# A chunked mLSTM with a four-expert layer behind it: small moves between engines and queues in the recurrence

## The chip, the cores and the metric

The kernel runs on one core of one Trainium2 chip. The metric is the device time of one execution in microseconds (us); lower is better. Three executions of the kernel before took 395.02, 394.61 and 394.67 us, median 394.67. One further execution was profiled.

## The reference

The first half is an mLSTM: for 2 batches and 8 heads, over 768 steps, with head size 40. With a running maximum m of the log gates:

```
m_new  = max(f + m, i);  fs = exp(f + m - m_new);  is = exp(i - m_new)
C = fs * C + is * v k^T;   n = fs * n + is * k
y = sigmoid(o) * (C q) / max(|n . q|, 1)
```

The 16 heads' outputs of a step are joined to a row x of 320 numbers; there are 1536 rows. The second half sends every row through four experts and adds them up with weights p, where p = domain_probs / (sum of domain_probs over the experts + 1e-9):

```
out = sum over e of  p[:, e] * (max(x @ w1[e], 0) @ w2[e])      # w1: 320 x 1024, w2: 1024 x 320
```

All is float32. The experts' matmuls keep that precision by splitting both operands into a high and a low part of a faster format and adding three products.

## The kernel before

The sequence is cut into 6 chunks of 128 steps, and one "pair" j is chunk j of both batches (n = 2j and 2j+1). Inside a chunk from the second on, the work goes in halves of 64 steps. The state of all heads is carried from half to half in small tiles cs. Each pair passes through the same functions:

- load_qk, load_vk, load_o and load_f fetch q and k, v and k, the output gates, and the forget factors, the last broadcast to 64 partitions from a copy in HBM, f_d. gate_o takes the sigmoid of the output gates, in place, on ScalarE.
- decay scans the factors to decay products (VectorE, L432); scores makes q.k (TensorE, L479); weigh multiplies both (VectorE, L497).
- values and keys scale v and k on GpSimd (L454, L458); state multiplies them on TensorE (L527); carry (GpSimd, L534) and keep (VectorE, L543) bring the state forward.
- inter multiplies q with the carried state (TensorE, L554) and scales the product by a factor of its row and head to yb; intra multiplies the weighed scores with v (L595).
- norms adds yb to intra's result in PSUM (L602), multiplies with the output gates (L606), divides (L610, L611 and L646 to L653); turn transposes the rows (TensorE, L661), and the result is split to high and low parts in xst (ScalarE L664, VectorE L668).

steps(n) interleaves n pieces of expert 0's matmuls (hidden, L157; output, L204) with this recurrence. After it the four experts run as a long stream of matmuls on TensorE, with 512 rows at a time, while the next expert's weights are loaded and split.

Every engine works through its own instructions in the order in which the Python code issues them; nothing is reordered. All loads and stores are issued from SyncE (SP), in code order too. A load that shall not start too early is held back by behind(ap): a tiny store to a scratch row `mark`, which waits until ap has been written, and everything after it on SP waits with it. Each transfer uses one of eight semaphores in turn, and waits until the transfer eight before it has landed.

The places touched by the change: the tile f_d (L266), its two stores (L770 to L774) and its reading (load_f, L428); the load of the domain weights pw (L775), their sum (L827 to L831) and their scaling (L849, L852); the load of the third pair's output gates (L819) and their sigmoid (L918); inter's scaling on VectorE, used for pair 1 only (L559 to L565); the scan of n = 5 (decay(5), L889), its keys (L890) and the mark before load_f(3) (L891).

Of the kernel before, what the change touches and what calls it, by code (L numbers as in the profile page):

```python
# [44 lines left out]
def tile_mlstm_moe(ctx, tc, g0, g1, qk, vk, ot, dp, w1, w2, out):  # L45
# [177 lines left out]
    with ExitStack() as actx:  # L223
# [39 lines left out]
        gl = gp.tile([L, S], F32, name="gl")  # L263
        tri = const.tile([L, 2, L], F32, name="tri")
        half = const.tile([L, 32], F32, name="half")
        f_d = dram.tile([B, 2 * (NC - 2), H * C], F32, name="f_d")  # L266
        mark = dram.tile([24, 32], F32, name="mark")
        marks = iter(range(24))
        ident = const.tile([L, L], F32, name="ident")
# [105 lines left out]
        def load_qk(j, c=None):  # L375
            c = slice(0, 2) if c is None else slice(c, c + 1)
            nc.sync.dma_start(qks[j % 2][:, c], qk[j, :, c])
# [7 lines left out]
        def load_o(j):  # L385
            nc.sync.dma_start(acc[:, 2 * j:2 * j + 2], ot[:, 2 * j:2 * j + 2])
# [34 lines left out]
        def load_f(j):  # L421
            for n in (2 * j, 2 * j + 1):
                b, c = n % B, n // B
                fbs[n] = fb = a0.tile([L, H, C], F32, tag="fb", name="fb")
                for u in range(2):
                    nc.sync.dma_start(
                        fb[hs[u]].rearrange("p h t -> p (h t)"),
                        f_d[b, 2 * (c - 2) + u:2 * (c - 2) + u + 1].to_broadcast([C, H * C]),  # L428
                    )

        def scan(out, f, i):
# [25 lines left out]
        def keys(n):  # L457
            nc.gpsimd.tensor_mul(  # L458
                kp[n % 2][:, :, 0:D], vks[n // 2][:, n % 2, 1],
                dds[n][:, :, (C if n // B else L) - 1:].to_broadcast([L, H, D]),  # L460
            )
# [49 lines left out]
        def cst(j, u):  # L511
            return cs[(2 * j + u) % 3]
# [19 lines left out]
        def carry(j, u):  # L532
            cd = cds[j, u] = a1.tile([104, B * NP, D + 1], F32, tag=f"cd{u}", name="cd")
            nc.gpsimd.tensor_mul(  # L534
                cd, cst(j, u)[0:104],
                bl[0:104, u, j].unsqueeze(2).to_broadcast([104, B * NP, D + 1]),
            )

        def keep(j, u):

            st, cd = sts[j][u], cds.pop((j, u))
            for q in rows:
                nc.vector.tensor_add(cst(j, u + 1)[q], cd[q], st[q, :, 0:D + 1])  # L543

        def inter(j, eng=nc.scalar):

            y1 = ps_a.tile([L, 2, B, NP, C], F32, tag="a", name="y1")
            for n in (2 * j, 2 * j + 1):
                b = n % B
                for p in range(NP):  # L550
                    for r in range(2):
                        q = slice(64 * r, 64 + D * r)
                        for u in (r, 1 - r):
                            nc.tensor.matmul(  # L554
                                y1[hs[u ^ r], r, b, p, 0:D + 1], qT(n)[q, p, hs[u]],
                                cst(j, u)[q, b * NP + p], start=True, stop=True,
                            )
            yb = ybs[j] = a1.tile([L, 2, B, NP, D + 1], F32, tag="yb", name="yb")
            if eng is nc.vector:  # L559
                eng.tensor_mul(  # L560
                    yb.rearrange("t r b p d -> t r (b p) d"),
                    y1.rearrange("t r b p d -> t r (b p) d")[..., 0:D + 1],
                    bT[:, :, j].unsqueeze(3).to_broadcast([L, 2, B * NP, D + 1]),
                )
                return  # L565
            for b in range(B):
                for p in range(NP):
                    for r in range(2):
                        i = b * NP + p
                        nc.scalar.activation(  # L570
                            yb[:, r, b, p], y1[:, r, b, p, 0:D + 1], AF.Copy,
                            scale=bT[:, r, j, i:i + 1],
                        )

        def intra0(b):
            pool, tag = (ps_a, "a") if b else (ps_h, "ph")
            y = ys[0, b] = pool.tile([L, 2, NP, C], F32, tag=tag, name="y0")
            for p in range(NP):
                for r in range(2):
                    h = 2 * p + r  # L580
                    for t in hs:
                        nc.tensor.matmul(
                            y[t, r, p, 0:D + 1], pms[b][:, h, t], vp[b][:, h, 0:D + 1],
                            start=True, stop=True,
                        )
# [107 lines left out]
        def decays(j):  # L693
            decay(2 * j)
            decay(2 * j + 1)
            if j + 1 < NG:
                load_f(j + 1)
# [3 lines left out]
        def steps(n):  # L701
            for _ in range(n):
                if not work[0].step():
                    work.pop(0)
# [62 lines left out]
        scores(1)  # L767
        gate_o(0)
        gate_starts(2, nc.gpsimd)
        for b in range(B):  # L770
            nc.sync.dma_start(  # L771
                f_d[b].rearrange("u (h t) -> h u t", h=H),
                fs[b * H:(b + 1) * H].rearrange("h (u t) -> h u t", t=C),
            )  # L774
        nc.sync.dma_start(pw, dp)  # L775
        load_w1(1)
        load_vk(1)
        load_qk(1, 1)
        intra0(0)
        quarter_hi(0)  # L780
        decay(1)
# [34 lines left out]
        )  # L816
        load_f(2)
        load_o(1)
        load_o(2)  # L819
        scores(3)  # L820
        values(2)
        keys(2)
# [1 line left out]
        quarter_lo(3, nc.vector)  # L824
        weigh(1)
        values(3)
        psum_e = const.tile([L, NCH, 1], F32, name="psum_e")  # L827
        nc.gpsimd.tensor_add(psum_e, pw[:, :, 0:1], pw[:, :, 1:2])
        for e in range(2, NE):
            nc.gpsimd.tensor_add(psum_e, psum_e, pw[:, :, e:e + 1])  # L830
        nc.gpsimd.tensor_scalar_add(psum_e, psum_e, 1e-9)  # L831
        keys(3)
        gate_b(1, NC, ps_o.tile([L, 512], F32, tag="po", name="pb"))
        bexp(1, NC)
# [11 lines left out]
        split_w2_lo(w2s, 4, 2, w2r, nc.gpsimd)  # L846
        state(1)
        keep(1, 0)
        nc.vector.reciprocal(psum_e, psum_e)  # L849
        carry(1, 1)  # L850
        split_w2_lo(w2s, 6, 2, w2r, nc.gpsimd)
        nc.gpsimd.tensor_mul(pw, pw, psum_e.to_broadcast([L, NCH, NE]))  # L852
        steps(1)
        gate_o(1)
        keep(1, 1)
# [7 lines left out]
        for j in range(1, NG):  # L863
            a, b = 2 * j, 2 * j + 1
            nxt, far = j + 1 < NG, j + 2 < NG
            k = SLOTS[j - 1]
            if j == NG - 2:
                raw1 = raws.tile([L, 3, FF], F32, tag="raw", name="raw1")

            def load(i, ap):  # L870
                if far or j == NG - 2:
                    behind(ap)
                if far:
                    (load_vk, None, lambda j: (load_qk(j), load_o(j)))[i](j + 2)
                elif j == NG - 2:
                    nc.sync.dma_start(raw1[:, i], w1[1, :, i])

            if nxt:
                values(a + 2)
                values(b + 2)  # L880
                if j > 1:
                    decays(j + 1)
                keys(a + 2)
                if j > 1:
                    keys(b + 2)
                steps(1)
            norm = norms(j)
            if j == 1:
                decay(5)  # L889
                keys(5)  # L890
                behind(dds[5][0:1, 0, 0:32])  # L891
                load_f(3)
            else:
                load(0, xms.pop(j)[0:1, 1, 0, 0:32])
                steps(1)
            norm(nc.vector if j == 1 else nc.gpsimd)
            if j == 1:
                steps(1)
            if nxt:
                carry(j + 1, 0)  # L900
            if j == 1:
                scores(a + 2)
                scores(b + 2)
                weigh(j + 1)
            steps(k[0] - 1 - nxt)
            if j > 1:
                turn(j)()
            if nxt:
                if j > 1:
                    gate_o(j + 1)  # L910
                if j > 1:
                    scores(a + 2)
                    scores(b + 2)
                hidden = work[0].todo[0][0] == work[0].hidden
                state(j + 1, *((ps_o, "po") if hidden else (ps_h, "ph")))
                if j == 1:
                    low = turn(j)
                    gate_o(j + 1)  # L918
                keep(j + 1, 0)
                if j == 1:  # L920
                    load(0, cst(j + 1, 1)[0:1, 0, 0:32])
                if not far:
                    load(1, cst(j + 1, 1)[0:1, 0, 0:32])
                low() if j == 1 else weigh(j + 1)
                if far:
                    carry(j + 1, 1)
                    keep(j + 1, 1)
                steps(k[1])
                inter(j + 1)
                load(2, ybs[j + 1][0:1, 0, 0, 0, 0:32])  # L930
                intra(j + 1)
# [113 lines left out]
```

## Time and profile before

| what | value |
|---|---|
| median of three executions | 394.67 us (394.61 to 395.02) |
| the profiled execution, its own time | 393.91 us |
| its span, first to last instruction | 392.3 us |
| mean granted TensorE clock | 0.998 |
| TensorE matmul (PE) busy | 385.1 us, 98% |
| TensorE weight load (PEld) busy | 350.7 us, 89% |
| VectorE (DVE), ScalarE (ACT), GpSimd (POOL) busy | 158.0, 122.1 and 93.9 us |
| transfers of queue q1 (data), q8 (instructions) | 27.95 MB, 0.46 MB |

Start times are counted from the first instruction of the span. The busy time of PE is modelled at its ends, so a busy PE may be a little less busy than the row says. "<-" in a row names what ended a wait; "issue" is a wait that ends with nothing that the profile records. The recurrence lies in the first 107 us; from there on the four experts' stream follows.

### The profile page before, as it was taken

The numbers are of one execution on the slowest core, as the hardware profiler recorded it, in microseconds if no ns is written. First come the engines' busy times: TensorE is split into PE (matmuls) and PEld (weight loads), VectorE is DVE, ScalarE is ACT, GpSimd is POOL, SyncE is SP. The second block draws the span as 40 slices with busy tenths as digits, with TensorE's granted clock in tenths as the row PEclk, the third lists the DMA queues.
The fourth block names the chain that finished last, engine by engine and source line by source line (L and its number), as shares of the span: only waits on it lengthen the run. The fifth ranks groups of instructions, "written<-read, shape, count | busy, mean of one in ns | idle before, by whom it ended". The sixth has DMA issues, their size and how long they took to land.

```text
span 392.3 us, 8240 instructions
## 1 busy us (share of the span) xinstructions
PE 385.1 (98%) x3584; PEld 350.7 (89%) x3584; DVE 158.0 (40%) x270; ACT 122.1 (31%) x288; POOL 93.9 (24%) x114
## 2 busy tenths in 40 slices
PE   9999899999999999999999999999999999999996
PEld 6899799999989989989889889889889899899896
DVE  7788867675423132142141251241231431321321
ACT  3773744446263231062130240160220420310310
POOL 8988444370453100034100010071000100000000
PEclk9999999999999999999999999999999999999999
DMA  6795654353003220003000040003000001001001
GB/s 248 238 319 192 195 191 155 111 198 97 16 1 134 62 100 2 0 2 134 0 2 0 2 160 2 0 1 135 0 2 0 2 2 49 17 17 52 0 18 50
DMA packets 8717, 28.46 MB, mean 73 GB/s; under 512 B 1354, under 2 KB 2906, under 8 KB 7530
## 3 DMA queue, kind: packets, MB, share of 16 engines
q1 hardware_dynamic: 8682, 27.95, 21.1%
q8 instruction: 28, 0.46, 0.5%
q14 instruction: 7, 0.06, 0.0%
HBM read 25.94 MB, written 2.00 MB: 71 GB/s over the span
## 4 chain that ended last, share of the span: by engine, by line
PE 91%; POOL 3%; DVE 2%; DMA 2%; issue 1%; SPq 1%; ACT 0%; POOLq 0%
PE po L204 43%; PE ph L157 39%; PE ph L187 3%; DMA qk<-in_qk 2%; PE y L595 1%; PE s L479 1%; PE y L554 1%; PE px L661 1%; PE st L527 1%; POOL tri L748 1%; POOL gl L289 0%; POOL xr L649 0%; SPq L771 0%; POOL gl L290 0%; POOL vp L454 0%
## 5 line engine op out<-in xcount | busy, mean ns | idle before, releaser
L204 PE MATMUL po<-w2s,h 128*128 128x320 f32 x1152 | 172.4, 309 | 0.0
L204 PEld LDWEIGHTS po<-w2s,h 128*128 128x128 f32 x1152 | 169.8, 188 | 1.0
L157 PE MATMUL ph<-xst,w1s 128*128 128x512 f32 (+1 forms) x816 | 163.0, 358 | 0.0
L157 PEld LDWEIGHTS ph<-xst,w1s 128*128 128x128 f32 x816 | 135.8, 189 | 24.2 <-issue 2.4
L166 ACT ACTIVATE h<-ph 128x512 fp32r<-128x512 f32 x96 | 57.4, 598 | 193.0 <-PE ph L157 191.3
L170 DVE SCALAR_TENSOR_TENSOR h<-ph,h 128x512 fp32r<-128x512 f32 x96 | 66.3, 691 | 106.9 <-ACT h L166 106.4
L215 DVE SCALAR_TENSOR_TENSOR acc<-po,pw,acc 128x320 f32<-128x320 f32 x36 | 19.8, 551 | 99.9 <-PE po L204 99.9
L92 POOL TENSOR_TENSOR w1s<-raw,w1s 128x512 fp32r<-128x512 f32 (+1 forms) x24 | 23.5, 1017 | 76.0 <-ACT w1s L89 70.9
L92 POOL TENSOR_TENSOR w2s<-raw,w2s 128x640 fp32r<-128x640 f32 x6 | 9.5, 1577 | 96.2 <-ACT w2s L89 96.2
L432 DVE TENSOR_TENSOR_SCAN dd<-fb,id 128x512 f32<-128x512 f32 x14 | 17.3, 1269 | 1.4 <-POOL kp L458 0.9
L89 ACT ACTIVATE w2s<-raw 128x640 fp32r<-128x640 f32 x12 | 8.8, 733 | 18.3 <-DMA raw<-in_w 18.3
L454 POOL TENSOR_TENSOR vp<-vk,iT 128x320 f32<-128x320 f32 x12 | 11.1, 944 | 9.1 <-PE y L595 4.2
L213 ACT ACTIVATE acc<-po,pw 128x320 f32<-128x320 f32 x12 | 6.3, 526 | 22.0 <-PE po L204 22.0
L570 ACT ACTIVATE yb<-y,bT 128x41 f32<-128x41 f32 x64 | 12.3, 343 | 2.0 <-PE y L554 2.0
L649 POOL TENSOR_TENSOR xr<-xm,ni 64x320 f32<-64x320 f32 x9 | 7.5, 836 | 20.9 <-DVE ni L611 20.6
L187 PE MATMUL ph<-xd,w1s 64*128 64x512 f32 x40 | 12.0, 420 | 0.0
L187 PE MATMUL ph<-xst,w1s 64*128 64x512 f32 x40 | 12.0, 418 | 0.0
L89 ACT ACTIVATE w1s<-raw 128x512 fp32r<-128x512 f32 (+1 forms) x24 | 11.2, 517 | 0.0
L458 POOL TENSOR_TENSOR kp<-vk,dd 128x320 f32<-128x320 f32 x12 | 9.8, 828 | 2.0 <-DVE y L610 1.9
L187 PEld LDWEIGHTS ph<-xst,w1s 64*128 64x128 f32 x40 | 6.6, 185 | 2.9 <-issue 1.9
L543 DVE TENSOR_TENSOR cs<-cd,st 40x328 f32<-40x328 f32 x18 | 8.8, 492 | 0.7 <-POOL cd L534 0.4
L92 DVE TENSOR_TENSOR w2s<-raw,w2s 128x640 fp32r<-128x640 f32 x6 | 5.3, 889 | 9.2 <-ACT w2s L89 9.2
(105 smaller groups left out, 202.2 us busy)
## 6 DMA issues: line engine op xcount, KB each, us to landing
qk<-in_qk SPq DMA_DIRECT2D x4, 1024.0 KB, 4.8
raw<-in_w SPq DMA_DIRECT2D x3, 1280.0 KB, 5.2
vk<-in_vk SPq DMA_DIRECT2D x5, 640.0 KB
raw<-in_w SPq DMA_DIRECT2D x2, 1536.0 KB
qk<-in_qk SPq DMA_DIRECT2D x4, 512.0 KB, 6.3
fb<-f_d SPq DMA_DIRECT2D x16, 128.0 KB, 5.5
acc<-in_ot SPq DMA_DIRECT2D x6, 320.0 KB, 6.5
out<-acc SPq DMA_DIRECT2D x12, 160.0 KB, 1.7
```

The lines of the kernel that those rows point to most:

```text
L89: nc.scalar.activation(hi, raw, AF.Copy)
L92: eng.tensor_sub(lo, raw, hi.bitcast(F32))
L157: nc.tensor.matmul(ph[:, i, :], self.w1s[:, wi, f * L:(f + 1) * L], xst[:, xi, self.t0:self.t0 + n], start=(k == 0 and not self.wide), sto ...
L166: nc.scalar.activation(hh, ph, AF.Relu)
L170: nc.vector.scalar_tensor_tensor(out=hl, in0=ph, scalar=0.0, in1=hh.bitcast(F32), op0=ALU.max, op1=ALU.subtract)
L187: nc.tensor.matmul(self.banks[f][:, 0, :], self.w1s[r, 5, f * L:(f + 1) * L], x, start=True, stop=False,)
L204: nc.tensor.matmul(po, self.hs[f][a][:, sl], ws[:, b, f, :], start=(first and i == 0), stop=(last and i == len(ks) - 1),)
L215: nc.vector.scalar_tensor_tensor(out=acc[:, i, :], in0=po, scalar=pw[:, i, e:e + 1], in1=acc[:, i, :], op0=ALU.mult, op1=ALU.add,)
L432: nc.vector.tensor_tensor_scan(out=out.rearrange("p h t -> p (h t)"), data0=f.rearrange("p h t -> p (h t)"), data1=i.rearrange("p h t -> p ...
L454: nc.gpsimd.tensor_mul(vv[:, :, 0:D], vks[n // 2][:, n % 2, 0], iec.to_broadcast([L, H, D]))
L458: nc.gpsimd.tensor_mul(kp[n % 2][:, :, 0:D], vks[n // 2][:, n % 2, 1], dds[n][:, :, (C if n // B else L) - 1:].to_broadcast([L, H, D]),)
L570: nc.scalar.activation(yb[:, r, b, p], y1[:, r, b, p, 0:D + 1], AF.Copy, scale=bT[:, r, j, i:i + 1],)
```

## The change

- f_d is laid out as (half chunk, all heads of both batches), and is stored with one transfer for both batches.
- The load of pw is issued after load_qk(1, 1), three loads later than before.
- pw's sum over the experts is one VectorE reduction instead of three small GpSimd additions, and the addition of 1e-9 and the final multiplication are on VectorE too, all beside the reciprocal that was already there.
- load_o(2) moves from the loads after load_f(2) to a place behind load_vk(3), in pass j = 1; gate_o(2) moves from pass j = 1 (after turn) to pass j = 2, ahead of norms(2).
- inter for pair 1 scales half of its product (r = 0) on VectorE and the other half with eight ScalarE activations.
- In pass j = 1, decay(5) comes ahead of keys(4), and so ahead of the addition in norms(1); keys(5) follows keys(4) directly, and the mark before load_f(3) waits for the keys of n = 5 instead of its scan.

```diff
-        f_d = dram.tile([B, 2 * (NC - 2), H * C], F32, name="f_d")
+        f_d = dram.tile([2 * (NC - 2), B * H * C], F32, name="f_d")
...
-                        f_d[b, 2 * (c - 2) + u:2 * (c - 2) + u + 1].to_broadcast([C, H * C]),
+                        f_d[2 * c - 4 + u:2 * c - 3 + u, b * H * C:(b + 1) * H * C].to_broadcast(
+                            [C, H * C]
+                        ),
...
             if eng is nc.vector:
                 eng.tensor_mul(
-                    yb.rearrange("t r b p d -> t r (b p) d"),
-                    y1.rearrange("t r b p d -> t r (b p) d")[..., 0:D + 1],
-                    bT[:, :, j].unsqueeze(3).to_broadcast([L, 2, B * NP, D + 1]),
-                )
-                return
+                    yb[:, 0].rearrange("t b p d -> t (b p) d"),
+                    y1[:, 0].rearrange("t b p d -> t (b p) d")[..., 0:D + 1],
+                    bT[:, 0, j].unsqueeze(2).to_broadcast([L, B * NP, D + 1]),
+                )
             for b in range(B):
                 for p in range(NP):
-                    for r in range(2):
+                    for r in range(eng is nc.vector, 2):
...
-        for b in range(B):
-            nc.sync.dma_start(
-                f_d[b].rearrange("u (h t) -> h u t", h=H),
-                fs[b * H:(b + 1) * H].rearrange("h (u t) -> h u t", t=C),
-            )
-        nc.sync.dma_start(pw, dp)
+        nc.sync.dma_start(
+            f_d.rearrange("u (g t) -> g u t", g=BH), fs.rearrange("g (u t) -> g u t", t=C)
+        )
         load_w1(1)
         load_vk(1)
         load_qk(1, 1)
+        nc.sync.dma_start(pw, dp)
...
         load_f(2)
         load_o(1)
-        load_o(2)
...
-        psum_e = const.tile([L, NCH, 1], F32, name="psum_e")
-        nc.gpsimd.tensor_add(psum_e, pw[:, :, 0:1], pw[:, :, 1:2])
-        for e in range(2, NE):
-            nc.gpsimd.tensor_add(psum_e, psum_e, pw[:, :, e:e + 1])
-        nc.gpsimd.tensor_scalar_add(psum_e, psum_e, 1e-9)
...
         keep(1, 0)
+        psum_e = const.tile([L, NCH, 1], F32, name="psum_e")
+        nc.vector.tensor_reduce(psum_e, pw, mybir.AxisListType.X, ALU.add)
+        nc.vector.tensor_scalar_add(psum_e, psum_e, 1e-9)
         nc.vector.reciprocal(psum_e, psum_e)
+        nc.vector.tensor_mul(pw, pw, psum_e.to_broadcast([L, NCH, NE]))
         carry(1, 1)
         split_w2_lo(w2s, 6, 2, w2r, nc.gpsimd)
-        nc.gpsimd.tensor_mul(pw, pw, psum_e.to_broadcast([L, NCH, NE]))
...
                 if j > 1:
                     decays(j + 1)
+                else:
+                    decay(b + 2)
                 keys(a + 2)
-                if j > 1:
-                    keys(b + 2)
+                keys(b + 2)
                 steps(1)
+            if j == 2:
+                gate_o(2)
             norm = norms(j)
             if j == 1:
-                decay(5)
-                keys(5)
-                behind(dds[5][0:1, 0, 0:32])
+                behind(kp[1][0:1, 0, 0:32])
                 load_f(3)
...
                 if j == 1:
                     low = turn(j)
-                    gate_o(j + 1)
                 keep(j + 1, 0)
                 if j == 1:
                     load(0, cst(j + 1, 1)[0:1, 0, 0:32])
+                    load_o(2)
```

## Rows read from the trace of the kernel before

**Rows 1.** The page: busy time by engine, and the queue that carries instructions.

```profile
PE 385.1 (98%) x3584; PEld 350.7 (89%) x3584; DVE 158.0 (40%) x270; ACT 122.1 (31%) x288; POOL 93.9 (24%) x114
...
q8 instruction: 28, 0.46, 0.5%
```

**Rows 2.** Waits of PE: engine, line, releaser; us in total, times, longest.

```profile
PE st L527 <- issue: 0.7, 1, 0.7
PE y L595 <- issue: 0.6, 1, 0.6
```

**Rows 3.** Timeline of PE: start, us, instructions, [idle before <- releaser].

```profile
22.37 0.69 PE L479 MATMUL s<-qk 64*64 64x64 f32 x32 [0.29 <-DMA qk<-in_qk]
...
41.25 0.42 PE L527 MATMUL st<-vp,kp 64*40 64x41 f32 x18 [0.74 <-issue]
41.60 0.87 PE L661 MATMUL px<-ident,xr 128*128 128x128 f32 x6
42.23 1.41 PE L204 MATMUL po<-w2s,h 128*128 128x320 f32 x8
43.57 1.14 PE L554 MATMUL y<-cs,qk 64*64 64x41 f32 x64
45.12 0.67 PE L595 MATMUL y<-vp,pm 64*64 64x41 f32 x30 [0.41 <-DVE xst L669]
46.36 0.72 PE L595 MATMUL y<-vp,pm 64*64 64x41 f32 x34 [0.57 <-issue]
```

**Rows 4.** The chain that ended last, 12 to 23 us: start, us, what.

```profile
12.93 1.22 SPq L771
...
14.19 0.36 SPq L775
...
16.05 6.27 DMA qk<-in_qk
```

**Rows 5.** Transfers of 38.8 to 39.9 us, in 40 slices and by queue.

```profile
DMA  0090000000000000000000000000000000000000
...
q8 instruction: 1, 0.02, 5.5%
```

**Rows 6.** Transfers of 43.9 to 45 us in 40 slices, GB/s.

```profile
GB/s 0 0 596 0 0 186 745 372 0 0 186 186 0 186 0 186 745 186 0 0 186 186 0 0 372 372 186 372 372 0 0 186 559 186 559 559 186 0 0 559
```

**Rows 7.** Transfers of 50.3 to 50.4 us, by queue.

```profile
q8 instruction: 1, 0.02, 60.1%
```

**Rows 8.** Stretches: us, PE, PEld, DVE, ACT, POOL busy, granted clock, DMA share, GB/s.

```profile
37.30:38.80 1.50, 1.50 (x12) 1.35 (x10) 1.50 (x2) 0.00 (x0) 0.01 (x1) 1.00 0.00 0
...
40.50:43.80 3.30, 2.56 (x49) 2.31 (x49) 2.95 (x6) 2.20 (x8) 1.61 (x3) 1.00 0.58 159
...
46.50:52.00 5.50, 5.50 (x75) 5.45 (x72) 3.99 (x6) 2.81 (x12) 3.49 (x4) 1.00 0.95 318
```

**Rows 9.** Timeline of DVE.

```profile
31.56 0.69 DVE L170 SCALAR_TENSOR_TENSOR h<-ph,h 128x512 fp32r<-128x512 f32 x1 [1.01 <-ACT h L166]
...
35.21 0.84 DVE L560 TENSOR_TENSOR yb<-y,bT 128x656 f32<-128x656 f32 x1
...
37.87 1.22 DVE L432 TENSOR_TENSOR_SCAN dd<-fb,id 128x512 f32<-128x512 f32 x1
...
51.42 0.81 DVE L606 TENSOR_TENSOR xm<-y,acc 128x640 f32<-128x640 f32 x1
```

**Rows 10.** Timeline of ACT.

```profile
44.84 3.07 ACT L570 ACTIVATE yb<-y,bT 128x41 f32<-128x41 f32 x16 [0.33 <-PE y L554]
```

**Rows 11.** Timeline of POOL.

```profile
35.21 1.40 POOL L454 TENSOR_TENSOR vp<-vk,iT 128x320 f32<-128x320 f32 x2
36.57 0.74 POOL L458 TENSOR_TENSOR kp<-vk,dd 128x320 f32<-128x320 f32 x1
```

**Rows 12.** Timeline of SP: issues of transfers.

```profile
39.40 2.37 SPq L426 DMA_DIRECT2D fb<-f_d  x4
...
43.07 0.36 SPq L383 DMA_DIRECT2D vk<-in_vk  x1
```

## The prediction

> **What bounds the kernel now.** I read the page first: TensorE's matmuls are busy 385.1 of 392.3 us [rows 1]. The change touches no matmul and no order of them, so whatever it can give lies in the few microseconds in which TensorE waits, and all of them fall in the recurrence. The second view is therefore the list of TensorE's own waits, in which two called "issue" stand out, 0.7 and 0.6 us [rows 2]. Third comes TensorE's timeline around them [rows 3].
>
> The timeline shows that the two "issue" waits are of one kind. Between the restart at 41.25 and the one at 46.36 TensorE ran 18 + 6 + 8 + 64 + 30 = 126 matmuls [rows 3], each with its weight load, so 252 instructions and a few waits. The instruction queue moved 0.46 MB in 28 packets, 16.4 KB each [rows 1]; TensorE's 7168 instructions over 28 are 256 for a packet. So TensorE stopped twice where a block of 256 instructions ended, and the next was not there. Fourth view, the transfers: one such packet starts in the third of 40 slices of 38.8 to 39.9, at 38.86 [rows 5], the next in the third slice of 43.9 to 45, at 43.96 [rows 6]; TensorE restarts 2.39 and 2.40 us after them. From the restart at 41.25 the loop is 2.71 us to the next packet and 2.40 to the next restart, 5.11 in all. The work of that stretch is less, so between 41.25 and 46.36 the refill of instructions sets the pace, and the 0.41 us spent there on VectorE's xst [rows 3] cost nothing. That is the frame of the sum: before 41 us a wait that goes is a gain, between 41 and 46 only a shorter refill is.
>
> The Trainium skill, page Runtime: NRT & Kernel Launch, section Instruction fetch mechanics, has blocks of 16 KiB or 256 instructions too, and says of the cost of crossing one: "mostly hidden". The blocks agree with the rows; at two of the crossings the cost is 0.74 and 0.57 us in plain sight, and the measurement decides.
>
> **The change part by part.**
>
> One store of the factors, and pw behind three loads: SP issued the second store in 1.22 us and pw in 0.36 [rows 4]. Behind them stood load_w1(1), load_vk(1) and load_qk(1, 1), the last issued at 16.05 and landed 6.27 later [rows 4], when TensorE had waited 0.29 us for it [rows 3]. The remaining store has twice the pieces; it takes between the time of one of the old and of both. So load_qk(1, 1) is issued between 0.36 and 1.58 us earlier, and either end covers the 0.29. All that stands ahead of it in the queue moves with it. **Gain 0.29 us.** Everything of TensorE up to the first "issue" wait then runs 0.29 earlier, since the timeline shows no other wait from 22.37 to 40.51.
>
> pw's sum and scaling: GpSimd loses five small instructions and VectorE gets three more. The trace has no such reduction; the nearest row is the multiply of 128x656 elements in 0.84 us [rows 9], and pw has 48 elements in a row. So three of them cost between nothing and 2.5 us, and I take 0.25 each, 0.75 in all, since the data is a fourteenth. They stand ahead of the low part at 31.56, before which VectorE was idle 1.01 us waiting for ScalarE [rows 9]: free at my value, and 1.5 us of delay at the far end, which could reach TensorE through the output matmuls that read that low part. GpSimd's release brings the weights' low parts earlier, for which nobody waits.
>
> Half of the scaling on ScalarE: VectorE's multiply falls from 0.84 [rows 9] to about half. ScalarE did 16 such activations in 3.07 us [rows 10], so eight are 1.54. It can start when VectorE can, at about 35, and is done by about 36.5. In VectorE's queue the scan of 1.22 [rows 9] now stands in that gap: 35.21 + 0.42 + 1.22 = 36.85, so the addition waits for no one. It comes 0.7 us later than before, but the scan no longer stands behind it, so the chain to the transpose ends about 0.4 earlier. The transpose at 41.60 followed the state matmuls without a wait [rows 3]: nothing gained, and if the cover is gone (ScalarE 0.4 late), nothing lost either.
>
> load_f(3): its mark followed the scan and was issued just before 39.40 [rows 12]. Now it follows keys(5) on GpSimd: the values from 35.21 take 1.40, two keys 0.74 each [rows 11], so 38.1, and 0.29 earlier with TensorE. The four loads thus start about 1.3 us earlier. Their transfers are what moves between 40.5 and 43.8, at a DMA share of 0.58 [rows 8], and they end just where the second refill's packet starts, 43.96 [rows 6]. This is my main choice: I read the 2.71 us of that refill as time spent behind them. A refill in a stretch with a share of 0.95 [rows 8] started at 50.3 [rows 7], 3.99 after the restart at 46.36; so traffic does lengthen it. With load_f(3) gone from 43.8 to 42.5, the packet can start at 42.7, TensorE can restart at 45.1, and it gets to the end of the block at 45.79 - 0.29 = 45.5. **Gain 0.57 us**, bounds 0 (the refill's trip doesn't change) and 0.57.
>
> load_o(2) and gate_o(2): 320 KB leave the loads behind load_f(2) and go behind load_vk(3), issued at 43.07 [rows 12]. The sigmoid is wanted by norms(2), whose multiply came at 51.42 [rows 9]. Issued about 43.5, in a queue behind 640 KB, it should land some 3 us ahead; VectorE's and ScalarE's work in between is what it was. Price zero; if it lands late, ScalarE stands and TensorE's next hidden bank with it.
>
> Sum on the profiled execution: 393.91 - 0.29 - 0.57 = 393.05, of which 1.6 us lie around the span. The three runs' median stands 0.76 above it, and I carry the difference over: 394.67 - 0.86 = 393.81, **393.8 us**.
>
> **The rivals.**
>
> The first refill becomes shorter as well. It was asked for when the block before it had arrived, and that one was fetched in a crowded stretch; with 320 KB less and earlier loads there, it can come a microsecond sooner. Then the 0.74 [rows 3] goes too: 394.67 - 0.29 - 0.74 - 0.57 = 393.07. Against it: the DMA share was 0.00 from 37.3 to 38.8 [rows 8], and the packet still started only at 38.86, so traffic alone did not hold it. Chance 0.2.
>
> Only the qk wait goes. The same idle stretch speaks for a trip of nearly fixed length, 2.6 to 2.7 us, whatever load_f(3) does. Then both issue waits stay: 394.67 - 0.29 = 394.38. Chance 0.27. By the Trainium skill, page DMA: Bandwidth & Descriptors, section Queues, rings and completion order, a DMA engine takes turns between its queues packet by packet; a refill would then wait for a packet and not for the rest of load_f(3), which is this rival and its time. The 3.99 against 2.71 us speaks against it.
>
> Nothing is gained: the refills absorb the 0.29, because the first was asked for at a time that TensorE's earlier start does not move, or load_qk(1, 1) lands as late as before in a queue that is full. 394.67. Chance 0.1.
>
> Slower: the second refill falls behind load_vk(3) and load_o(2). Place: the block end near 45.5. VectorE is free earlier, so load_vk(3) is issued perhaps 0.8 us earlier, and its packets start at 43.2; before, they came just behind the refill's packet [rows 6]. If that packet has not started by then, it shares a full queue as the one at 50.3 did, and its 2.71 us become 3.99: 1.28 more, less 0.29, makes 394.67 + 0.99 = 395.66. It decides from the point where the packet starts later than load_vk(3). Against it: load_f(3)'s transfers clear the queue 0.7 us ahead. Chance 0.13, and 0.05 for the other slips of this sign (the sums on VectorE at their far end, the gates late).
>
> **How the numbers follow.** The forecast has 0.25, the shorter first refill 0.2, the qk wait alone 0.27, nothing 0.1, slower 0.18. About 0.2% or 0.79 us is what a measurement of this kernel tells from no change, and the forecast lies only just beyond it: of its 0.25 I count 0.2 as faster and 0.05 as the same. Faster: 0.2 + 0.2 + a little of the mixed cases between the first two rivals, 0.03, so 0.43. Same: 0.05 + 0.24 + 0.1, so 0.39. Slower: 0.18. The range reaches from 392.8, below the time of the shorter first refill with the medians' own scatter, to 395.2, within the slower case; about 1 in 10 is left out on each side. The likeliest one's own range is 393.5 to 394.2.
>
> **What would show it.** Right: TensorE's wait for qk is gone; of the two issue waits the second is gone and the first is as long as before, 0.3 us earlier; load_f(3) is issued near 38.1; the instruction packet that started at 43.96 starts near 42.7. VectorE's low part of the last hidden bank ends before 32.3, and nothing waits for the gates. Wrong: a second issue wait of 0.5 us or more with its packet 2.7 us behind the restart (the fixed trip), a packet behind load_vk(3) (the slower case), or a new TensorE wait on VectorE between 28 and 36 us. If no wait of TensorE has changed and the time has, the frame itself is wrong.

## The result and the profile after

The changed kernel took 396.21 us (median of nine executions, 394.69 to 397.11) against 394.02 us for the kernel before (nine, 393.13 to 395.02), side by side on one chip. The ratio is 1.0051, with a 95% interval of 1.0031 to 1.0071: half a percent slower. The forecast was 393.8 us, the range ended at 395.2.

The span of the profiled execution grew from 392.3 to 394.5 us. The line of busy times, which answers to [rows 1], says where not to look: TensorE's work is almost the same.

```profile
PE 385.8 (98%) x3584; PEld 350.9 (89%) x3584; DVE 160.4 (41%) x273; ACT 123.7 (31%) x296; POOL 91.4 (23%) x109
```

The list of TensorE's waits after, to be held against [rows 2] (engine, line, releaser; us in total, times, longest):

```profile
PE st L529 <- issue: 1.9, 1, 1.9
PE po L204 <- DVE h L170: 1.2, 1, 1.2
...
PE po L204 <- issue: 0.3, 1, 0.3
```

The wait for qk is gone, and so is the second "issue" wait. The first one, 0.74 before, has become two, 0.27 and 1.85. And there is a wait that the kernel before does not have: the output matmuls of the hidden step wait 1.24 us for VectorE's low part, h. TensorE's timeline after, to be held against [rows 3]:

```profile
22.37 0.69 PE L481 MATMUL s<-qk 64*64 64x64 f32 x32
...
30.68 2.07 PE L204 MATMUL po<-w2s,h 128*128 128x320 f32 x13
34.00 0.70 PE L204 MATMUL po<-w2s,h 128*128 128x320 f32 x3 [1.24 <-DVE h L170]
34.63 1.14 PE L556 MATMUL y<-cs,qk 64*64 64x41 f32 x64
...
38.20 2.65 PE L204 MATMUL po<-w2s,h 128*128 128x320 f32 x17 [0.27 <-issue]
40.78 1.16 PE L481 MATMUL s<-qk 64*64 64x64 f32 x64
...
44.30 0.42 PE L529 MATMUL st<-vp,kp 64*40 64x41 f32 x18 [1.85 <-issue]
...
48.16 1.14 PE L596 MATMUL y<-vp,pm 64*64 64x41 f32 x64 [0.40 <-DVE xst L670]
49.24 8.06 PE L157 MATMUL ph<-xst,w1s 128*128 128x256 f32 x64
```

Starts of the same work in the two profiles show where the time came in:

| work of TensorE | before | after | later by |
|---|---|---|---|
| output matmuls of the hidden step, first | 30.68 | 30.68 | 0 |
| inter for pair 1 | 33.12 | 34.63 | 1.51 |
| scores, L479 / L481 | 38.84 | 40.78 | 1.94 |
| 47th state matmul, behind the issue wait | 41.25 | 44.30 | 3.05 |
| intra, L595 / L596 | 45.12 | 48.16 | 3.04 |
| next hidden matmuls, L157 | 47.01 | 49.24 | 2.23 |

So +1.51 at the new wait, +0.43 at the small issue wait, +1.11 at the large one, and -0.81 where the second issue wait used to be. The sum is 2.23 us (a hundredth is rounding), and the spans differ by 2.2. Nothing after 50 us counts.

Why the low part came late is in VectorE's timeline (start, us, what):

```profile
30.32 0.20 DVE L843 TENSOR_REDUCE psum_e<-pw 128x12 f32<-128x48 f32 x1
30.56 0.41 DVE L844 TENSOR_SCALAR psum_e<-psum_e 128x12 f32<-128x12 f32 x1
31.00 0.23 DVE L845 RECIPROCAL psum_e<-psum_e 128x12 f32<-128x12 f32 x1
31.27 1.95 DVE L846 TENSOR_TENSOR pw<-pw,psum_e 128x48 f32<-128x48 f32 x1
33.25 0.69 DVE L170 SCALAR_TENSOR_TENSOR h<-ph,h 128x512 fp32r<-128x512 f32 x1
```

The low part began at 31.56 before [rows 9] and at 33.25 now, right behind a multiplication of 48 elements in a row that took 1.95 us; the reduction of the same 48 took 0.20. GpSimd's timeline at that time:

```profile
29.36 1.58 POOL L92 TENSOR_TENSOR w2s<-w2r,w2s 128x640 fp32r<-128x640 f32 x1 [0.20 <-ACT w2s L89]
30.90 0.74 POOL L536 TENSOR_TENSOR cd<-cs,bl 104x328 f32<-104x328 f32 x1
31.60 1.56 POOL L92 TENSOR_TENSOR w2s<-w2r,w2s 128x640 fp32r<-128x640 f32 x1
```

GpSimd's split ends at 33.16, VectorE's multiplication at 33.22. The addition of 1e-9 shows the same in small: 0.41 us, ending at 30.97, when the split before it had ended at 30.94. So the reading that the experiments had to test: VectorE's multiplication was held out while GpSimd worked. It is called the lockout from here on.

The Trainium skill, page SBUF — State Buffer, section Who interferes with whom, has this rule: a VectorE instruction with both inputs in SBUF, or one in a two-port mode, which a tensor_scalar can enter, shares a pair of ports with GpSimd's reads, and the later of the two stands until the other is through; a reduction does not. The rows agree for the multiplication, the addition and the reduction. I had not weighed this rule in the forecast.

### The profile page after: what moved, and what is told of

It is laid out like the page before. It is cut to its first block, busy times and chain, and to the rows that moved or that the text cites. A ratio compares the mean times of both kernels' runs of the same rounds, so it can differ in the third digit from the quotient of the medians.

```text
span 394.5 us, 8244 instructions
## 1 busy us (share of the span) xinstructions
PE 385.8 (98%) x3584; PEld 350.9 (89%) x3584; DVE 160.4 (41%) x273; ACT 123.7 (31%) x296; POOL 91.4 (23%) x109
## 4 chain that ended last, share of the span: by engine, by line
PE 93%; DVE 4%; issue 2%; ACT 1%; POOL 0%; POOLq 0%; ACTq 0%; DVEq 0%
PE po L204 42%; PE ph L157 39%; PE ph L187 3%; PE s L481 1%; PE y L596 1%; PE pwm L71 1%; PE y L556 1%; PE px L662 1%; PE fb L416 1%; PE st L529 1%; DVE dd L434 1%; DVE h L170 1%; POOL xr L650 0%; DVE xm L607 0%; DVE pm L489 0%
## 5 line engine op out<-in xcount | busy, mean ns | idle before, releaser
L157 PE MATMUL ph<-xst,w1s 128*128 128x512 f32 (+1 forms) x816 | 163.1, 358 | 0.0
L157 PEld LDWEIGHTS ph<-xst,w1s 128*128 128x128 f32 x816 | 135.8, 189 | 24.3 <-issue 2.4
L92 POOL TENSOR_TENSOR w1s<-raw,w1s 128x512 fp32r<-128x512 f32 (+1 forms) x24 | 23.6, 1030 | 76.1 <-ACT w1s L89 70.9
L92 POOL TENSOR_TENSOR w2s<-raw,w2s 128x640 fp32r<-128x640 f32 x6 | 9.5, 1576 | 96.2 <-ACT w2s L89 96.2
L571 ACT ACTIVATE yb<-y,bT 128x41 f32<-128x41 f32 x72 | 13.9, 340 | 5.4 <-DVE yb L562 3.2
L536 POOL TENSOR_TENSOR cd<-cs,bl 104x328 f32<-104x328 f32 x9 | 6.8, 757 | 11.1 <-DVE cs L545 10.8
```

The source lines that it names most:

```text
L92: eng.tensor_sub(lo, raw, hi.bitcast(F32))
L157: nc.tensor.matmul(ph[:, i, :], self.w1s[:, wi, f * L:(f + 1) * L], xst[:, xi, self.t0:self.t0 + n], start=(k == 0 and not self.wide), sto ...
L571: nc.scalar.activation(yb[:, r, b, p], y1[:, r, b, p, 0:D + 1], AF.Copy, scale=bT[:, r, j, i:i + 1],)
```

## The experiments

Each is timed against the kernel before in the same batch; its median was 394.04 us for the first four, 393.66 for the next four and 393.96 for the last three.

**e1: the multiplication back on GpSimd.**

```diff
-        nc.vector.tensor_mul(pw, pw, psum_e.to_broadcast([L, NCH, NE]))
         carry(1, 1)
         split_w2_lo(w2s, 6, 2, w2r, nc.gpsimd)
+        nc.gpsimd.tensor_mul(pw, pw, psum_e.to_broadcast([L, NCH, NE]))
```

> The changed kernel, with one instruction put back: pw's final multiplication by the reciprocal of its sum runs on GpSimd again, behind the last of the weights' low parts. Theory A (the multiply on VectorE stood behind GpSimd's subtractions, 1.95 us at 31.27, and made the low part of the last hidden bank late; TensorE's 1.24 us wait for it then made the refills of instructions late too): the low part starts before 31.7, TensorE has no wait at the output matmuls, the two or three issue waits sum to at most 1.3 us, and the time is 393.2 to 394.0, at or below the kernel before. Theory B (the first refill, 1.85 us, is late because load_qk(2) and load_f(3) are moved at the same time): only the 1.24 goes, the long issue wait stays above 1.5 us, and the time is 394.8 to 395.3.

Measured 394.46 us (393.36 to 397.18), ratio 1.0016 (0.9994 to 1.0039): most of the loss is gone, but three of twelve executions lie near 397, and the median lies between the times of the two theories. The profile is one of the three (396.94). VectorE there:

```profile
30.18 2.87 DVE L844 TENSOR_SCALAR psum_e<-psum_e 128x12 f32<-128x12 f32 x1
...
33.35 0.69 DVE L170 SCALAR_TENSOR_TENSOR h<-ph,h 128x512 fp32r<-128x512 f32 x1
```

and GpSimd:

```profile
26.20 4.62 POOL L92 TENSOR_TENSOR w2s<-w2r,w2s 128x640 fp32r<-128x640 f32 x3
30.79 0.73 POOL L536 TENSOR_TENSOR cd<-cs,bl 104x328 f32<-104x328 f32 x1
31.48 1.54 POOL L92 TENSOR_TENSOR w2s<-w2r,w2s 128x640 fp32r<-128x640 f32 x1
```

Now the addition, 12 elements in a row, took 2.87 us and ended at 33.05, with GpSimd's last split at 33.02. It was held across two changes from one GpSimd instruction to the next, so the price can be the rest of GpSimd's unbroken run and not only of one instruction. It need not be: in the changed kernel the same addition got in at such a change, at 30.94. The low part is as late as in the changed kernel, by the other instruction. The same profile shows a second cost (us, busy times, granted clock, DMA share, GB/s):

```profile
35.41:42.24 6.83, 6.83 (x113) 6.75 (x106) 5.78 (x10) 3.19 (x16) 4.55 (x6) 0.50 0.43 162
```

TensorE had waited 1.73 us for h up to 34.10; from 35.41 it was granted half its clock, 1.2 of 2.4 GHz, for 6.83 us.

**e2: the multiplication on VectorE, but behind keep(1, 1).**

```diff
-        nc.vector.tensor_mul(pw, pw, psum_e.to_broadcast([L, NCH, NE]))
...
         keep(1, 1)
+        nc.vector.tensor_mul(pw, pw, psum_e.to_broadcast([L, NCH, NE]))
```

> The changed kernel, with the final multiplication of pw still on VectorE, but issued after keep(1, 1), when the low part is done and GpSimd has no work on the weights. Theory A: the same instruction takes 0.2 to 0.4 us there instead of 1.95, and the time is that of the variant with the multiply on GpSimd, 393.2 to 394.0. Theory C (the multiply is slow on VectorE in itself, by its broadcast operand): about 1.9 us again, now ahead of decay(4), and the time stays above 395.

Measured 393.80 us (393.15 to 396.75), ratio 1.0006 (0.9985 to 1.0026).

```profile
31.68 0.69 DVE L170 SCALAR_TENSOR_TENSOR h<-ph,h 128x512 fp32r<-128x512 f32 x1 [0.33 <-ACT h L166]
...
33.31 0.21 DVE L851 TENSOR_TENSOR pw<-pw,psum_e 128x48 f32<-128x48 f32 x1
```

The same instruction costs 0.21 us where GpSimd rests, a ninth of 1.95. The low part starts at 31.68, held only by ScalarE, and no output matmul waits. The loss is gone; no gain stands in its place.

**e3: only the sums.** The kernel before, with all of pw's sums on VectorE as in the change and nothing else changed.

```diff
-        nc.gpsimd.tensor_add(psum_e, pw[:, :, 0:1], pw[:, :, 1:2])
...
+        nc.vector.tensor_reduce(psum_e, pw, mybir.AxisListType.X, ALU.add)
+        nc.vector.tensor_scalar_add(psum_e, psum_e, 1e-9)
         nc.vector.reciprocal(psum_e, psum_e)
+        nc.vector.tensor_mul(pw, pw, psum_e.to_broadcast([L, NCH, NE]))
```

> The kernel before, with one part of the change: pw's sum, 1e-9 and multiplication on VectorE, beside the reciprocal. Theory A: the multiply again takes 1.5 to 2 us and TensorE waits about 1.2 us for the low part; the refills come later, and the time is 1.2 to 2.4 us above the kernel before. Theory B: 1.2 us above it at most, with issue waits as before (0.7 and 0.6). If the sums are not the cause: no change.

Measured 395.81 us (395.22 to 396.39), ratio 1.0044 (1.0027 to 1.0062): this part alone brings nearly the whole loss, 1.77 of 2.19 us, as theory A had it. TensorE's timeline has the same two long waits:

```profile
34.06 0.70 PE L204 MATMUL po<-w2s,h 128*128 128x320 f32 x3 [1.29 <-DVE h L170]
...
43.99 0.42 PE L527 MATMUL st<-vp,kp 64*40 64x41 f32 x18 [1.73 <-issue]
```

The second issue wait is gone here too, although load_f(3) stands where it stood.

**e4 and e5: the sum in PSUM.** psum_e becomes 12 columns of a PSUM tile that is there anyway, so the multiplication keeps its place but has only one input in SBUF. e5 adds an unused tile of psum_e's size, 48 bytes in each partition, so that the other tiles stay where they were.

```diff
-        gate_b(1, NC, ps_o.tile([L, 512], F32, tag="po", name="pb"))
+        pb1 = ps_o.tile([L, 512], F32, tag="po", name="pb")
+        gate_b(1, NC, pb1)
...
-        psum_e = const.tile([L, NCH, 1], F32, name="psum_e")
+        psum_e = pb1[:, 400:400 + NCH].unsqueeze(2)
+        const.tile([L, NCH, 1], F32, name="unused")     # e5 only
```

> The changed kernel, with the sum of pw and its reciprocal in unused columns of the PSUM tile of gate_b, so that the multiply has one operand in SBUF and one in PSUM; order and engine are those of the changed kernel. Theory A in its exact form (two SBUF operands of VectorE and GpSimd's reads exclude one another): the multiply takes 0.2 to 0.4 us in the same place, the low part starts before 31.9, and the time is 393.2 to 394.2. If the multiply waits for something else there (its instructions, its place, the reciprocal): 1.5 to 2 us again and a time of 396.

> As e4 (sum and reciprocal of pw in PSUM, everything else as in the changed kernel), but the 48 bytes per partition that the sum no longer needs in SBUF stay allocated, so that every other tile lies where it does in the kernel before. In e4 the hidden stages of experts 1 and 3 took 13.2 us instead of 12.8 and hid what the sums gave. Theory A: the multiply takes 0.2 to 0.4 us in the old place, TensorE doesn't wait for the low part, the hidden stages take 12.8 us, and the time is 393.2 to 394.2. If the PSUM operands themselves made the stream slow: 13.2 again and 396.

VectorE in e5, and GpSimd at the same time:

```profile
28.94 0.99 DVE L545 TENSOR_TENSOR cs<-cd,st 40x328 f32<-40x328 f32 x2
...
30.21 0.18 DVE L846 TENSOR_SCALAR pb<-pb 128x12 f32<-128x12 f32 x1
...
30.70 0.20 DVE L848 TENSOR_TENSOR pw<-pw,pb 128x48 f32<-128x48 f32 x1
31.21 0.69 DVE L170 SCALAR_TENSOR_TENSOR h<-ph,h 128x512 fp32r<-128x512 f32 x1 [0.30 <-ACT h L166]
```

```profile
26.22 4.63 POOL L92 TENSOR_TENSOR w2s<-w2r,w2s 128x640 fp32r<-128x640 f32 x3
```

The addition decides it. With its operand in PSUM it took 0.18 us and ended at 30.39, while GpSimd's splits ran on to 30.85; with its operand in SBUF it had taken 0.41 and 2.87 us. keep(1, 0), with one input in SBUF (cd) and one in PSUM (st), was not held by the same splits either: two of them took 0.99 us from 28.94. The multiplication, 0.20 us instead of 1.95, agrees, but by itself it does not tell: it now began at 30.70 and ended 0.05 us behind the splits' end. So where the inputs lie decides whether VectorE is held out. The runs show the exclusion and what lifts it, not what lies behind it. e5 took 393.69 us (393.20 to 396.18), ratio 1.0014 (0.9999 to 1.0029), level with before.

e4 had the same fast multiplication and yet took 396.17 us (395.35 to 399.09), ratio 1.0053 (1.0027 to 1.0079). The loss moved: of the long stream's hidden stages some became slower. The chain that ended last, e4 (start, us, what):

```profile
109.19 12.92 PE ph L157 x56
...
137.32 13.27 PE ph L157 x56
```

and e5:

```profile
136.59 12.96 PE ph L157 x56
...
164.76 12.92 PE ph L157 x56
```

With the 48 bytes restored the stages are 12.92 to 12.96 again, so the place of the tiles behind psum_e, all that differs between e4 and e5, made the 0.31 to 0.35 us a stage. Why they do is open.

**e6: all four sums on VectorE behind keep(1, 1).** **e7: e6, with load_qk(2) issued directly behind load_vk(2).** For e7:

```diff
         load_vk(2)
+        load_qk(2)
...
-        load_qk(2)
```

> The changed kernel, with all four instructions on pw's sum (reduce, 1e-9, reciprocal, multiply) still on VectorE, but behind keep(1, 1), while GpSimd is idle. Theory A: each takes 0.2 to 0.25 us, no execution meets a VectorE instruction held up by GpSimd, the time is 393.2 to 393.9 without executions above 395. Theory B (the rest of the change costs time by its transfers): above 394.4.

> As e6, with load_qk(2) (1 MB) issued directly behind load_vk(2), some 5 us earlier, so that it no longer moves between 33 and 37 us, where the instruction refill before the first issue wait is asked for. If refills are held up by transfers: its packet starts 1 us or more earlier (before 38), the first issue wait falls below 0.3, and the time is 0.4 to 1.0 us below e6. If a refill takes its 2.6 to 3.1 us whatever moves: the issue wait stays at 0.7 to 1.1 and the time is that of e6.

e6 took 393.62 us (392.89 to 398.42), ratio 1.0016 (0.9992 to 1.0041). The median is as expected, and the four instructions took 0.17 to 0.23 us each; but three executions lie above 396, where none was expected above 395. The profile is one of them (398.42), and shows how far the refills can go; TensorE's waits:

```profile
PE st L529 <- issue: 2.4, 1, 2.4
PE y L596 <- issue: 1.2, 1, 1.2
...
PE po L204 <- issue: 0.8, 1, 0.8
```

e7 took 392.77 us (392.37 to 394.73), ratio 0.9984 (0.9970 to 0.9998), and has no issue wait. TensorE's waits:

```profile
PE px L662 <- DVE xr L650: 0.5, 1, 0.5
PE y L596 <- DVE xst L670: 0.5, 1, 0.5
```

So moving load_qk(2), 1 MB, takes the first issue wait away. In the kernel before, an instruction packet started at 33.25, that load's transfers moved from 33.5 to 37.0, and the next packet started 5.61 us later, at 38.86 [rows 5]. In the changed kernel the packets started at 35.05 and 41.45, 6.40 apart, with most of the load from 35.3 to 38.5. In e7 they were 34.09 and 37.43, 3.34 apart, with the load all but past.

That the load moves behind a packet is not enough, though. In e1, which has it in the late place, the packet started at 34.94, the load moved from 35.4 to 38.8, and the next packet came 3.58 us later, at 38.52, without an issue wait. In the other eight profiles with the late place (before, after, e2 to e6, e8) packet and load start within 0.3 us of each other, and the next packet comes 5.4 to 8.1 us later. What stretches the refill is open.

**e8: shifted blocks.** The kernel before without two of its warm-up matmuls, which the page counts as four (3580 matmul instructions instead of 3584); one execution.

```diff
-WARM = (512, 512, 64)
+WARM = (512, 512)
...
-        keep_warm(256, ps_o, "po")
```

> The kernel before without two of its four warm-up matmuls, which are four matmuls and four weight loads, 8 instructions, at the very start. If the two issue waits are refills at the ends of blocks of 256 instructions, they move 4 matmuls to the back: behind the 50th matmul of the state group instead of the 46th, and behind the 34th of the intra group instead of the 30th. If they wait for something of the recurrence, they stay behind the 46th and the 30th.

It took 394.35 us.

```profile
39.97 0.71 PE L527 MATMUL st<-vp,kp 64*40 64x41 f32 x50
42.31 0.36 PE L527 MATMUL st<-vp,kp 64*40 64x41 f32 x14 [1.63 <-issue]
```

The wait moved from behind the 46th state matmul to behind the 50th, by the 4 that are missing. So the first issue wait does sit on the border of a block of 256 TensorE instructions. The second does not appear in this profile, so its shift could not be seen. And the first is 1.63 us here, where it had been 0.74, with every load in its old place: its length changes from one execution to another.

**e9: the kernel before with only load_qk(2) early** (the move of e7). **e10: the changed kernel with the same move.** **e11: e10, with pw's sums and multiplication on GpSimd (the latter behind the keys of n = 5) and pair 1's scaling whole on VectorE.**

> The kernel before with nothing of the change, but load_qk(2) issued directly behind load_vk(2). If the refills before both issue waits were held up by load_qk(2), the issue waits (0.7 and 0.6 us) both fall below 0.2 and the time is 0.6 to 1.2 us below the kernel before, about 392.8. If the gain of e7 came from the rest of the change: no difference from the kernel before.

> The changed kernel as it is, its multiply held up by GpSimd included, with load_qk(2) issued directly behind load_vk(2). This splits the loss: TensorE's direct wait for the low part (1.2 us) should stay, the issue waits (0.3 and 1.9) should go. If the loss is the direct wait plus refills that load_qk(2) holds up: 393.3 to 394.3, 2 to 3 us below the changed kernel. If the refills were late only because of the direct wait: the long issue wait stays above 1 us and the time above 395.

> A version put together: the changed kernel with load_qk(2) behind load_vk(2), pw's sums on GpSimd in their old place, the final multiply on GpSimd behind the keys of n = 5, and pair 1's scaling all on VectorE again (ScalarE's half waited for VectorE's half, so it was not beside it). Store, scan order, load_f(3) and load_o(2) are those of the change. Against e7 (392.8) it should lose the 0.5 us wait of the transpose for VectorE: 392.2 to 392.8. If that wait stays or the refills come back: 392.8 or more.

| run | median, us (lowest to highest) | ratio (95%) |
|---|---|---|
| e9 | 393.22 (392.36 to 393.93) | 0.9980 (0.9966 to 0.9993) |
| e10 | 395.83 (393.65 to 397.91) | 1.0043 (1.0017 to 1.0069) |
| e11 | 392.93 (392.28 to 394.08) | 0.9979 (0.9967 to 0.9992) |

e9's timeline of TensorE, to be held against [rows 3]:

```profile
39.77 0.84 PE L527 MATMUL st<-vp,kp 64*40 64x41 f32 x64
41.12 0.84 PE L661 MATMUL px<-ident,xr 128*128 128x128 f32 x6 [0.51 <-DVE xr L649]
```

Both issue waits are gone, with load_f(3) unmoved; the transpose now waits 0.51 us for VectorE, which the issue wait had covered. 0.74 + 0.57 - 0.51 is 0.80 us, and the medians differ by 0.74. e10 keeps the sums on VectorE and keeps the loss, though no issue wait is left, and neither of its two expectations describes that. Five of its executions lie at 393.65 to 394.23 with a mean clock of 0.999 and more, level with before and not below it as e9 and e11; seven lie at 395.55 to 397.91 with 0.991 to 0.996. Its profile is of the second kind. VectorE:

```profile
33.02 0.93 DVE L845 TENSOR_SCALAR psum_e<-psum_e 128x12 f32<-128x12 f32 x1
...
34.24 1.96 DVE L847 TENSOR_TENSOR pw<-pw,psum_e 128x48 f32<-128x48 f32 x1
```

TensorE, and the stretch behind its wait:

```profile
31.30 3.69 PE L157 MATMUL ph<-xst,w1s 128*128 128x256 f32 x16 [2.87 <-DVE h L170]
```

```profile
31.32:34.73 3.41, 3.41 (x16) 3.41 (x17) 3.26 (x7) 0.94 (x2) 3.41 (x4) 0.50 0.86 293
```

A wait of 2.87 us, then 3.41 us at half the clock. The multiplication is held out again, but this wait came ahead of it: the raw second weights landed only at 28.5 us, ScalarE waited 4.10 us for them, and the hidden step's activation stood behind its split. Why that load was late, and whether the other six slower executions are of this kind, is open; e10 does not separate the lockout's price from it. e11 has no lockout at the sums and is about as fast as e7 and e9; 392.8 at most had been expected. The transpose's wait for VectorE is gone, as expected, but the list of TensorE's waits has an issue wait again, at the border one block earlier:

```profile
PE po L204 <- issue: 0.5, 1, 0.5
```

So the early load does not take away every issue wait. e11 also undoes the split scaling and is no slower for that than e7.

## Why the prediction was wrong

**The step that failed** is pw's sum and scaling: "three of them cost between nothing and 2.5 us, and I take 0.25 each". The reduction and the addition took 0.20 and 0.41 us; the multiplication took 1.95. I had scaled it by its elements from a row in which one input, y, lies in PSUM [rows 9], and had not looked at what stood beside it. GpSimd's timeline before had it in plain sight:

```profile
28.77 3.12 POOL L92 TENSOR_TENSOR w2s<-w2r,w2s 128x640 fp32r<-128x640 f32 x2
31.83 0.76 POOL L534 TENSOR_TENSOR cd<-cs,bl 104x328 f32<-104x328 f32 x1
32.52 1.58 POOL L92 TENSOR_TENSOR w2s<-w2r,w2s 128x640 fp32r<-128x640 f32 x1
```

VectorE's timeline before had the effect itself: the same split of 64x256 (L92) took 0.42 us at 24.66 and 0.94 at 21.48, where GpSimd's vp ran until 22.15.

The far end I had named, 1.5 us of delay that reaches TensorE through the output matmuls, is what happened: 1.51 us. I gave it, with the gates, a chance of 0.05. e2, e3 and e5 show the mechanism three ways: the multiplication moved, the sums alone, and the sums in place with psum_e out of SBUF.

**The second failure** is what follows from a late start. I treated the refills as a frame that a delay cannot lengthen. But they moved with it, the packet at 33.25 to 35.05 and the one at 38.86 to 41.45, so the first issue wait did not absorb the delay: 0.43 + 1.11 us came on top of the 1.51, less the 0.81 of the second wait that went. That the delay made the waits longer is not shown: with load_qk(2) in its late place the first issue wait is 1.0 to 2.4 us in e2, e4, e5, e6 and e8 too, where nothing was late. In four of the nine executions (396.85 to 397.11 us) the mean clock was 0.991 to 0.995, against 0.999 to 1.0 in the others (394.69 to 396.21). I had no term for the clock.

**The refills' cause was read wrongly.** I read the second refill as held up by load_f(3) and took the trip of the first for fixed, since the DMA share was 0.00 from 37.3 to 38.8 [rows 8]. e9 leaves load_f(3) in its place and loses both waits. The traffic that counted lay earlier: load_qk(2), from 33.5 to 37.0, which began with the packet before. So the rival of a shorter first refill named a real gain and the wrong lever; and with the lockout taken away the changed kernel (e2, e5, e6) gains nothing that can be measured: its first issue wait is 1.0 us in e2 and 1.2 in e5, where it had been 0.74. Nor was load_f(3) 1.3 us earlier: it was issued at 40.45 in the changed kernel, and at 39.07 and 38.59 in e2 and e5, against 39.40. GpSimd's values, which I priced at 1.40 us [rows 11], took 2.32 in the changed kernel:

```profile
36.41 2.32 POOL L456 TENSOR_TENSOR vp<-vk,iT 128x320 f32<-128x320 f32 x2 [3.25 <-PE y L596]
```

Beside them ran VectorE's moved scan, from 36.55, for 1.66 us instead of 1.22 [rows 9]. In e3, with the scan in its old place, they took 1.41. That this is the lockout again fits the rows; no run tests it by itself.

**What held.** The wait for qk is gone. Its gain shows only where the first transposes come early: they start at 15.28 to 15.40 us in five of the nine profiles with the new order of loads, where the scores start at 21.99 to 22.06; in the other four they start at 15.77 to 15.90, and the scores at 22.37 to 22.52, where the wait had put them before. The changed kernel's profile is one of these four: 22.37 again. The border of 256 instructions holds for the first issue wait (e8). The gates are free: their sigmoid ran at 51.95, and the multiplication that wants it at 53.66. The second issue wait did go, but not by the part that I credited (e3). Half of the scaling on ScalarE is worth nothing, as said, though not by the path that I gave; ScalarE waited for VectorE's half:

```profile
36.73 1.60 ACT L571 ACTIVATE yb<-y,bT 128x41 f32<-128x41 f32 x8 [3.15 <-DVE yb L562]
```

**The slower rival** that I worked out, a second refill behind load_vk(3) and load_o(2), did not happen: the packet at 45.94, behind load_vk(3), is followed by no issue wait, and the loss lies ahead of it.

## What to carry to other kernels

Before a small operation goes to VectorE, look at what GpSimd does at that moment: with its inputs in SBUF it can cost the rest of GpSimd's unbroken run, however few its elements. A place where GpSimd rests makes it cheap again (0.21 instead of 1.95 us for the multiplication), and so does an operand in PSUM (0.18 instead of up to 2.87 for the addition). On a kernel whose TensorE is nearly full, do not count on a later wait to absorb a delay: here 1.5 us at one wait came out as 2.2 us in the span, since the refills moved along with it and one of them took longer, for a reason that is open. Look for a TensorE "issue" wait's cause in the traffic around the packet before, not only around the one that came late; issuing one 1 MB load at 27.84 instead of 32.57 us (e9) gave 0.2%.

## What was not expected of the hardware

- From one instruction packet to the next it took 5.4 to 8.1 us where a 1 MB load began with the first of them, and 3.3 to 3.9 us where the load had been issued early (e7, e9 to e11) or began 0.5 us behind the packet (e1). TensorE stood up to 2.4 us for it.
- Waits of TensorE of 1.73 us (e1), 2.87 (e10) and 1.21 (e6, up to 66.18) were followed by 6.83, 3.41 and 3.41 us at half the granted clock, but not every wait was: the changed kernel's profile has waits of 1.24 and 1.85 us and a clock of 1.000, and e6's own wait of 2.40 us was followed by the full clock. What decides is open.
- An address shift of 48 bytes in each partition changed some stages of 56 hidden matmuls from 12.92 or 12.96 to 13.27 us (e4, e5).
